# Sums of x stored halfway between steps, four first products of expert 0 made ahead of the groups, weight sums placed behind a group's first product

## The chip, the core and the metric

The kernel runs on one core of a Trainium2 chip. The metric is the device time of one execution in microseconds (us). The kernel before the change took 2215.28 us (median of 3 runs, 2215.21 to 2216.24).

## The reference, cut to what matters

Three stages follow each other. All numbers are float32.

```python
# 1. delta-rule attention, 32 heads, 768 steps, head size 48 -> x [3072, 384]
# 2. mixture of 8 experts, dense, weighted by a balanced table P
logits = x @ w_gate;  P = exp(logits - logits.max())
for _ in range(8):
    P /= P.sum(1, keepdims=True) + 1e-09      # rows
    P /= P.sum(0, keepdims=True) + 1e-09      # columns
    P *= N / E
for e in range(E):
    h = np.maximum(x @ w1[e], 0.0)            # 384 -> 1024
    out += P[:, e:e+1] * (h @ w2[e])          # 1024 -> 384
# 3. h = x @ w_in;  out = (h * cos(h)) @ w_out   (384 -> 2048 -> 384)
```

## The kernel before, in words

**Precision.** Each float32 factor is split into two rounded parts (hi, lo), and a product is three or four matmuls of 128x128 weights by 512 tokens. So TensorE has most of the work.

**Attention and expert 0.** The function `tick` walks through strings of letters (`SEQ`), one letter per piece of work, in the order in which the engines get them. A letter `m` is a half step of expert 0: `moe0_h(s)` (nine matmuls into one bank, then `relu_split`: ScalarE rounds, VectorE subtracts) or `moe0_y(s)` (nine matmuls into the three banks `yb`). These halves stand in the list `mq`. When attention ends, 14 are left: a loop issues nine of them with the first steps of the balancing of P (`sk_some`), and five go into the groups.

**Groups.** Experts 1 to 7 run over pairs of token blocks: three pairs (p), 28 groups each, 84 groups (n) in all. Instead of x the groups use seven tiles T0 to T6 of sums and differences of x's blocks. `group(n)` makes seven products (`mm`, four matmuls each: T0 and T5 first, into banks A_ and G_, then T4, T1, T3, T2, T6) and four small ones (`zz`, with the third part of T1 or T6), copies banks on ScalarE, and makes four relus. Between them, at four places `F()`, it issues one piece of nine matmuls into `yb` from the groups before. After the first of these, `gates` reads the three banks `yb` on VectorE, multiplies by the expert's row of P, and GpSimd adds the result to the accumulator.

**Weights of the next group.** `s_prep(n + 1)` gives six steps q0 to q5: q0 is four sums on GpSimd (lines 1042 to 1045), q1 to q3 and q5 round on ScalarE and subtract on VectorE, q4 is four sums on GpSimd.

**Hand-over.** In the last group of a pair (n = 27 and 55) each T tile is loaded anew behind its last product (`tl`, `t_load`). All these loads go through SyncE's queue, in the order in which the code issues them, with the raw weights of the group after the next (`g_load`, lines 1007 and 1008).

**Sums of x.** `t_prep(p)` makes the T tiles of a pair and stores them to `tsc`. Its steps k0 to k7 load parts of x, add, subtract, and `emit` (ScalarE rounds into slot 4, line 897; VectorE puts the rest into slot 5, line 898). What a step makes is stored only when the next step begins (line 956), right ahead of that step's own work; a last empty step stores what is left. For p = 0 the steps are in `tq`, popped by `tick` at every fourth letter; for p = 1 and 2 they are in `bgq`, which a group pops at three places (`bg`): after the second `zz`, ahead of q5, and at its end. Each step is followed by an empty place. Behind them `bgq` holds 32 conversions of the last stage's weights (`cv`): p0 loads (lines 1160, 1163), two empty places, then p1, p2, p3 on VectorE (lines 1167 to 1179), and p3 stores to `wsn` (lines 1184 to 1191).

Of the kernel before, what the change touches and what calls it, by code (L numbers as in the profile page):

```python
# [9 lines left out]
F32R = mybir.dt.float32r  # L10
# [25 lines left out]
def kernel(  # L36
# [13 lines left out]
    nc = tc.nc  # L50
# [575 lines left out]
    def moe0_h(s):  # L626
        m, f = divmod(s, FT)

        bank = pa[0] if scr and s % 2 and not grp else hb
        h_mms(bank, f // 2, f, xb[m], 0, 512)  # L630
        h = hp.tile([128, 2, 512], F32R, tag="h", name="h")
        relu_split(h, bank, 512)
        h0_t[s] = h

# [10 lines left out]
    NS0 = NB * FT  # L645
# [6 lines left out]
    with tc.manual_schedule():  # L652
# [108 lines left out]
        n = [gk_n(2, pcd)]  # L761
# [17 lines left out]
        nc.scalar.activation(out=wg[:, :, 0, :], in_=wg_sb, func=ACTF.Copy)  # L779


        scr, grp = [], []

        mq = [(2, lambda: moe0_h(0))]
        for s in range(NS0):
# [6 lines left out]
        def half():  # L792
            if mq and mq[0][0] <= done[0]:
                mq.pop(0)[1]()
# [9 lines left out]
        def tick(u, seq):  # L804
            early = u < 2
            for x, c in enumerate(seq.split()):
                inv_some(3)
                if x % 4 == 3 and tq:
                    tq.pop(0)()
                if len(c) == 2:  # L810
                    u, c = int(c[1]), c[0]
                if c == "m":
                    half()
                elif c == "K":
                    pe_KS(u)
                elif c == "k":
                    pe_QS(u)
                elif c in "ZY":
                    pe_Z1(u, *([p01[:, 0]] if early else []))
                elif c in "zy":  # L820
                    pe_Z2(u, *([p01[:, 1]] if early else []))
                elif c == "U":
                    pe_U(u)
                    load_v(u + 2)
                elif c == "S":
                    pe_S(u)
                    load_k(u + 5)
                elif c == "P":
                    pe_PU(u)
                elif c == "T":  # L830
                    n = take(c)
                    if n is not None:
                        pe_TK(n)
                elif c == "B":
                    n = take(c)
                    if n is not None:
                        pe_GK(n)
                elif c == "N":
                    n = take(c)
                    if n is not None:  # L840
                        pe_N(n)
                elif c == "Q":
                    n = u if early else u + 1
                    if n < NU:
                        pe_TQ(n, p23 if early else pcd)
                        load_q(n + 1)
                elif c == "q":
                    n = u if early else u + 1
                    if n < NU:
                        pe_GQ(n, p01 if early else pab)  # L850
                elif c == "E":
                    pe_TQ(u)
                    load_q(u + 1)
                elif c == "e":
                    pe_GQ(u)
                elif c == "X":
                    pe_XT(u, p23 if early else pcd)
                    done[0] = u + 1
                elif c == "r" and u + 1 < NU:
                    inv_some(99)  # L860
                    inv_dm(Xsys)
                elif c == "R" and u + 1 < NU:
                    inv_tx(Xsys)
                elif c == "i" and u + 2 < NU:
                    inv_q.extend(inv_ops(Nst, Nsys, Xsys, tmp, nc.gpsimd))
                elif c in "Gg":
                    (pe_gate if c == "G" else pe_gate2)((u - 1) // 2)
                elif c in "ab":
                    w_half(0, "ab".index(c))
                    if c == "b":  # L870
                        w_load(1)
                elif c == "W":
                    n = take(c)
                    w_split(n)
                    if n + 1 < NG:
                        w_load(n + 1)
# [9 lines left out]
        def t_prep(p, sl, add):  # L886

            b0, b1 = 2 * p, 2 * p + 1
            s = [sl(i) for i in range(6)]
            g, v, later = add, nc.vector.tensor_tensor, []  # L890

            def ld(i, b, a, k):
                nc.sync.dma_start(out=s[i], in_=xs(b, a, k))

            def emit(i, src):
                hi, lo = s[4].bitcast(F32R), s[5].bitcast(F32R)
                nc.scalar.activation(out=hi, in_=src, func=ACTF.Copy)
                v(out=lo, in0=src, in1=hi.bitcast(F32), op=ALU.subtract)
                later.append((tsc[p][i, :, 0, :], s[4]))
                later.append((tsc[p][i, :, 1, :], s[5]))  # L900

            def corr(i, a, b, op, slot):
                o = s[slot].bitcast(F32R)
                v(out=o, in0=a, in1=b, op=op)
                later.append((tsc[p][i, :, 2, :], s[slot]))
                return o.bitcast(F32)

            def k0():
                ld(0, b1, 0, 0), ld(1, b1, 1, 0), ld(2, b0, 0, 0), ld(3, b0, 1, 0)

            def k1():
                g(out=s[0], in0=s[0], in1=s[1], op=ALU.add)
                g(out=s[2], in0=s[2], in1=s[3], op=ALU.add)
                ld(1, b1, 0, 1), ld(3, b1, 1, 1)

            def k2():
                v(out=s[2], in0=s[0], in1=s[2], op=ALU.subtract)
                emit(3, s[2])
                g(out=s[1], in0=s[1], in1=s[3], op=ALU.add)
                ld(3, b0, 1, 1)  # L920

            def k3():
                v(out=s[0], in0=s[1], in1=s[0], op=ALU.subtract)
                emit(5, s[0])
                ld(0, b0, 0, 1)

            def k4():
                v(out=s[1], in0=s[1], in1=s[2], op=ALU.subtract)
                emit(4, s[1])
                g(out=s[0], in0=s[0], in1=s[3], op=ALU.add)  # L930
                ld(2, b0, 1, 2), ld(3, b1, 1, 2)

            def k5():
                v(out=s[0], in0=s[0], in1=s[1], op=ALU.subtract)
                emit(2, s[0])
                ld(0, b0, 0, 2), ld(1, b1, 0, 2)

            c = {}

            def k6():  # L940
                for i, j in ((1, 0), (6, 1)):
                    o = s[j].bitcast(F32R)
                    nc.scalar.activation(out=o, in_=s[j], func=ACTF.Copy, scale=1.0 / 4096)
                    later.append((tsc[p][i, :, 2, :], s[j]))
                    c[i] = o.bitcast(F32)
                c[3] = corr(3, s[3], s[2], ALU.subtract, 4)

            def k7():
                corr(5, c[6], s[3], ALU.subtract, 5)
                c[4] = corr(4, c[6], c[3], ALU.subtract, 3)  # L950
                corr(2, c[1], c[4], ALU.subtract, 2)

            def step(f):
                def run():
                    for o, i in later:
                        nc.sync.dma_start(out=o, in_=i)
                    later.clear()
                    f()
                return run

            return [step(f) for f in (k0, k1, k2, k3, k4, k5, k6, k7, lambda: None)]

        tick(0, SEQ[0])
        tick(2, SEQ[1])
# [163 lines left out]
        sq = s_prep(0)  # L1128
        lead = [[], [], [], [sq[0]], [sq[1]], [sq[2]], [sq[3]], [sq[4]], [sq[5]]]
        nb = 0  # L1130
        while len(mq) > 5:
            for x in lead.pop(0) if lead else []:
                x()
            half()
            nb += 1
            if nb in (1, 2, 4, 6, 8):
                sk_some()
# [145 lines left out]
        def group(n):  # L1283
# [10 lines left out]
            def tl(i):  # L1294
                if swap:
                    t_load(p + 1, i)
# [8 lines left out]
            tl(0)  # L1305
            if n and n + 2 < NGR:
                g_load(n + 2)
            mm(G_, n, 5, True)
            tl(5)
            copy(B_, A_)  # L1310
            while late and late[0][0] <= n:
# [2 lines left out]
            skp(n)  # L1314
            gates()
            copy(s7, G_)
            nx[0]()
            mm(A_, n, 4)
            tl(4)
            if last:  # L1320
# [193 lines left out]
                net_b3(j - 1)  # L1514


        grp.append(1)
        skb[0] = hb
        for bank in (B_, D_):
            nc.tensor.matmul(  # L1520
                out=bank, lhsT=s_hi(0, 0), rhs=Tt[0][:, 0, :], start=True, stop=True, skip_group_check=True
            )
        fill.extend(lambda: half() for _ in range(len(mq)))
        group(0)
        tpv = tpt.rearrange("p a (s c) -> p (a s) c", c=512)
        for p in range(1, NP):
            for x in t_prep(p, lambda i: tpv[:, i, :], nc.gpsimd.tensor_tensor):
                bgq.extend([x, lambda: None])
        bgq.extend(cv)
        for n in range(1, NGR):  # L1530
            group(n)
# [69 lines left out]
```

## Time and profile before

| | value |
|---|---|
| median of 3 runs | 2215.28 us |
| the profiled execution's own time | 2210.57 us |
| its span, first to last instruction | 2208.9 us |
| TensorE busy | 2129.0 us, 96% of the span |
| VectorE, ScalarE, GpSimd busy | 1432.6, 997.5, 1087.2 us |
| TensorE busy in 400 to 600 us (end of attention, first groups) | 187.4 of 200 us |
| TensorE busy in 800 to 1600 us (groups, two hand-overs) | 793.5 of 800 us |

The page gives busy times over the whole span. Since TensorE is busy 96% of it, what matters is where it is not: the waits of TensorE by the line that waits and what released it, and in the timeline what stood in the way there. A matmul's record overlaps the next one's, so a row of eight matmuls that takes 1.98 us gives them 0.23 us each. The same row with a longer time shows matmuls at the lower granted clock: in 480 to 490 us the mean granted clock is 0.83 of full speed, in 490 to 500 us it is 1.00.

### The profile page before, as it was taken

The numbers are of one execution on the slowest core, as the hardware profiler recorded it, in microseconds if no ns is written. First come the engines' busy times: TensorE is split into PE (matmuls) and PEld (weight loads), VectorE is DVE, ScalarE is ACT, GpSimd is POOL, SyncE is SP. The second block draws the span as 40 slices with busy tenths as digits, with TensorE's granted clock in tenths as the row PEclk, the third lists the DMA queues.
The fourth block names the chain that finished last, engine by engine and source line by source line (L and its number), as shares of the span: only waits on it lengthen the run. The fifth ranks groups of instructions, "written<-read, shape, count | busy, mean of one in ns | idle before, by whom it ended". The sixth has DMA issues, their size and how long they took to land.

```text
span 2208.9 us, 40836 instructions
## 1 busy us (share of the span) xinstructions
PE 2129.0 (96%) x16359; PEld 1778.2 (81%) x16359; DVE 1432.6 (65%) x2289; ACT 997.5 (45%) x1819; POOL 1087.2 (49%) x1507
## 2 busy tenths in 40 slices
PE   6889999889999999999999999999999999999998
PEld 5677777677878888788888887888888888888888
DVE  6555544376566777677777776777776546666665
ACT  2333332244444444444444444444444446666665
POOL 4656544426655556565555565655555532222221
PEclk8889999999999999999999999999999999999999
DMA  4432323544442224522222236222222260000000
GB/s 85 103 81 67 81 57 91 189 173 128 138 137 95 71 92 119 199 91 92 92 87 89 71 116 217 90 79 92 91 82 74 67 271 17 13 29 29 15 15 15
DMA packets 217374, 206.66 MB, mean 94 GB/s; under 512 B 83952, under 2 KB 193040, under 8 KB 217184
## 3 DMA queue, kind: packets, MB, share of 16 engines
q1 hardware_dynamic: 213840, 197.16, 28.8%
q0 software_dynamic: 2176, 6.60, 0.9%
q8 instruction: 128, 2.10, 0.4%
q14 instruction: 62, 0.51, 0.1%
q10 hardware_dynamic: 1168, 0.30, 0.1%
HBM read 156.71 MB, written 47.28 MB: 92 GB/s over the span
## 4 chain that ended last, share of the span: by engine, by line
PE 84%; DVE 7%; DMA 4%; ACT 2%; issue 2%; POOL 1%; SPq 1%; DVEq 0%; POOLq 0%; ACTq 0%
PE ps L145 31%; PE ps L1212 22%; PE ps L1459 9%; PE ps L1418 8%; PE ps L133 4%; PE ps L1217 3%; DMA T<-tsc 2%; PE ps L459 1%; PE ps L273 1%; PE ps L247 1%; DVE mh L152 1%; PE ps L441 1%; PE ps L429 1%; PE ps L487 1%; DMA tsc<-tp 0%
## 5 line engine op out<-in xcount | busy, mean ns | idle before, releaser
L145 PE MATMUL ps<-mh,w2t 128*128 128x512 f32 x3024 | 742.5, 390 | 0.6 <-DVE ct L1248 0.5
L145 PEld LDWEIGHTS ps<-mh,w2t 128*128 128x128 f32 x3024 | 568.6, 188 | 120.8 <-DVE ct L1248 2.9
L1212 PE MATMUL ps<-T,w1t 128*128 128x512 f32 x2352 | 594.3, 392 | 10.7 <-DMA T<-xsc 4.8
L1212 PEld LDWEIGHTS ps<-T,w1t 128*128 128x128 f32 x2352 | 443.0, 189 | 106.1 <-ACT ps L1222 5.9
L1249 POOL TENSOR_TENSOR accp<-accp,ct 128x512 f32<-128x512 f32 x252 | 327.3, 1328 | 329.8 <-DVE ct L1248 329.7
L152 DVE SCALAR_TENSOR_TENSOR mh<-ps,mh 128x512 fp32r<-128x512 f32 x168 | 115.2, 686 | 264.4 <-ACT mh L151 264.4
L1222 ACT ACTIVATE ps<-ps 128x512 f32<-128x512 f32 x168 | 97.8, 582 | 309.5 <-PE ps L1212 238.2
L1248 DVE TENSOR_TENSOR ct<-ps,scr 128x512 f32<-128x512 f32 x252 | 158.2, 683 | 81.6 <-PE ps L145 78.3
L1222 ACT ACTIVATE ct<-ps 128x512 f32<-128x512 f32 x168 | 100.5, 598 | 244.0 <-PE ps L1212 243.9
L1427 POOL TENSOR_SCALAR tp<-tp 128x512 f32<-128x512 f32 x96 | 60.1, 626 | 247.2 <-ACT tp L1426 247.0
L1079 POOL TENSOR_TENSOR w1t<-w1t 128x128 fp32r<-128x128 f32 x84 | 62.9, 749 | 222.8 <-DVE w1t L1065 204.4
L1441 DVE TENSOR_TENSOR tp<-tp,ps 128x512 f32<-128x512 f32 x96 | 66.1, 688 | 144.8 <-ACT tp L1440 144.8
L151 ACT ACTIVATE mh<-ct 128x512 fp32r<-128x512 f32 x168 | 106.1, 632 | 101.9 <-DVE ct L1347 56.7
L152 DVE SCALAR_TENSOR_TENSOR mh<-ct,mh 128x512 fp32r<-128x512 f32 x168 | 144.6, 861 | 0.4 <-ACT mh L151 0.3
L1459 PE MATMUL ps<-w1t,h 128*128 128x384 f32 x600 | 136.8, 341 | 4.3 <-DVE h L1451 2.8
L133 PE MATMUL ps<-xb,w1t 128*128 128x512 f32 x432 | 116.4, 413 | 6.1 <-ACT xb L539 2.7
L1217 PE MATMUL ps<-T,w1t 128*128 128x512 f32 x336 | 118.8, 393 | 1.7 <-DMA T<-tsc 1.7
L1459 PEld LDWEIGHTS ps<-w1t,h 128*128 128x128 f32 x600 | 107.2, 189 | 12.5 <-DVE h L1451 5.4
L145 PE MATMUL ps<-h,w2t 128*128 128x512 f32 x432 | 113.2, 407 | 0.0
L352 POOL TENSOR_TENSOR w1t<-w1t 128x30 f32<-128x30 f32 (+9 forms) x180 | 99.1, 551 | 14.1
L133 PEld LDWEIGHTS ps<-xb,w1t 128*128 128x128 f32 x432 | 80.9, 194 | 26.8 <-DVE xb L540 3.5
L151 ACT ACTIVATE mh<-ps 128x512 fp32r<-128x512 f32 x168 | 98.5, 587 | 0.6 <-PE ps L1217 0.6
(272 smaller groups left out, 3445.8 us busy)
## 6 DMA issues: line engine op xcount, KB each, us to landing
scr<-in_moe_w_dram SPq DMA_DIRECT2D x84, 384.0 KB
raw<-in_moe_w_dram SPq DMA_DIRECT2D x84, 384.0 KB
wsn<-tp SPq DMA_DIRECT2D x64, 192.0 KB
scr<-pts SPq DMA_DIRECT2D x45, 256.0 KB
xsc<-xb SPq DMA_DIRECT2D x24, 384.0 KB
T<-tsc SPq DMA_DIRECT2D x12, 768.0 KB
tsc<-tp SPq DMA_DIRECT2D x28, 256.0 KB
tp<-xsc SPq DMA_DIRECT2D x24, 256.0 KB
```

What stands on the lines that cost most here:

```text
L133: nc.tensor.matmul(out=ps[:, :nn], lhsT=w[:, a, kk, fs], rhs=x[:, b, kk, c0:c0 + nn], start=(i == 0), stop=(i == 3 * KD - 1),)
L145: nc.tensor.matmul(out=banks[kd], lhsT=w[:, a, f % 2, kd * 128:(kd + 1) * 128], rhs=h[:, b, :], start=(first and b == 0 and a == 0), stop= ...
L151: nc.scalar.activation(out=h[:, 0, :nn], in_=ps[:, :nn], func=ACTF.Relu)
L152: nc.vector.scalar_tensor_tensor(out=h[:, 1, :nn], in0=ps[:, :nn], scalar=0.0, in1=h[:, 0, :nn].bitcast(F32), op0=ALU.max, op1=ALU.subtract,)
L352: eng.tensor_tensor(out=xsys[:, j + 1:, 0:j], in0=xsys[:, j + 1:, 0:j], in1=a, op=ALU.add)
L1212: nc.tensor.matmul(out=bank, lhsT=a, rhs=b, start=start and q == 0, stop=stop and q == 3, skip_group_check=True)
L1217: nc.tensor.matmul(out=bank, lhsT=s_z(n, f), rhs=Tt[(1, 6)[t]][:, 2, :], start=False, stop=True, skip_group_check=True)
L1222: nc.scalar.activation(out=out, in_=in_, func=ACTF.Copy)
L1248: nc.vector.tensor_tensor(out=c, in0=yb[kd], in1=pslot[t], op=ALU.mult)
L1249: nc.gpsimd.tensor_tensor(out=a[:, kd, :], in0=a[:, kd, :], in1=c, op=ALU.add)
L1418: nc.tensor.matmul(out=hb2(i), lhsT=net_w1(f, a, kk), rhs=x2[b](c, kk), start=(j == 0), stop=(j == 3 * KD - 1))
L1459: nc.tensor.matmul(out=ybk[t][:, :DM], lhsT=h[:, a, ts], rhs=net_w2(f, c), start=(f == 0 and j == 0), stop=(f == FT2 - 1 and j == 2),)
```

## The change

- `t_prep` no longer stores at the start of the next step: every step is followed by a `flush` of its own that issues the stores. `tick` pops at every second letter in place of every fourth; in `bgq` the flush takes the empty place.
- The 14 halves left of expert 0 are put in another order: the last four first products (s = 44 to 47) come ahead of the groups, each into a bank of its own, with their h in the groups' tiles `mh`; what is left for the groups is five second halves.
- In `group`, q0 (`nx[0]`) moves from behind `gates` to the place between the group's first and second product. The first product into bank D_ that only opens the bank (`seed`) moves from ahead of group 0 into it.

```diff
-        bank = pa[0] if scr and s % 2 and not grp else hb
+        if s >= NS0 - 4:
+            bank, h = (pa[2], pa[1], pa[0], hb)[s % 4], htile()
+        else:
+            bank = pa[0] if scr and s % 2 else hb
+            h = hp.tile([128, 2, 512], F32R, tag="h", name="h")
         h_mms(bank, f // 2, f, xb[m], 0, 512)
-        h = hp.tile([128, 2, 512], F32R, tag="h", name="h")
...
-                if x % 4 == 3 and tq:
+                if x % 2 == 1 and tq:
                     tq.pop(0)()
...
-            def step(f):
-                def run():
-                    for o, i in later:
-                        nc.sync.dma_start(out=o, in_=i)
-                    later.clear()
-                    f()
-                return run
-
-            return [step(f) for f in (k0, k1, k2, k3, k4, k5, k6, k7, lambda: None)]
+            def flush():
+                for o, i in later:
+                    nc.sync.dma_start(out=o, in_=i)
+                later.clear()
+
+            return [x for f in (k0, k1, k2, k3, k4, k5, k6, k7) for x in (f, flush)]
...
+        z = NS0 - 8
+        order = [("y", z), ("h", z + 2), ("y", z + 1), ("h", z + 3), ("y", z + 2)]
+        order += [("h", s) for s in range(NS0 - 4, NS0)] + [("y", s) for s in range(z + 3, NS0)]
+        mq[:] = [(0, lambda c=c, s=s: (moe0_h if c == "h" else moe0_y)(s)) for c, s in order]
         while len(mq) > 5:
...
+            nx[0]()
             mm(G_, n, 5, True)
+            if n == 0:
+                seed(D_)
             tl(5)
...
             copy(s7, G_)
-            nx[0]()
             mm(A_, n, 4)
...
             for x in t_prep(p, lambda i: tpv[:, i, :], nc.gpsimd.tensor_tensor):
-                bgq.extend([x, lambda: None])
+                bgq.append(x)
         bgq.extend(cv)
```

**Place one: SyncE's queue at the first hand-over (group 27).** `T_6388` is T0, `T_6389` T5, `T_6390` T4, `T_6391` T3, `T_6392` T2, `T_6393` T1, `T_6394` T6; `wsn` are the stores of a conversion's p3, `tp<-in_moe_w` the load of a p0, `scr` and `raw` a group's raw weights. Before:

```order
L1189 DMA wsn_76<-tp 128x384 x2
L1094 DMA T_6388<-xsc_71 128x2x512
L1099 DMA T_6388<-xsc_71 128x512
L1007 DMA raw_6400<-in_moe_w_dram 128x3x256
L1008 DMA raw_6400<-in_moe_w_dram 128x2x384
L1101 DMA T_6389<-tsc_96 128x1536
L1101 DMA T_6390<-tsc_96 128x1536
L1163 DMA tp<-in_moe_w_out_dram 128x768
L1101 DMA T_6391<-tsc_96 128x1536
```

And of the change, at the same place:

```order
L1008 DMA scr<-in_moe_w_dram 128x2x384
L1094 DMA T_6388<-xsc_71 128x2x512
L1099 DMA T_6388<-xsc_71 128x512
L1007 DMA raw_6400<-in_moe_w_dram 128x3x256
L1008 DMA raw_6400<-in_moe_w_dram 128x2x384
L1101 DMA T_6389<-tsc_96 128x1536
L1101 DMA T_6390<-tsc_96 128x1536
L1101 DMA T_6391<-tsc_96 128x1536
```

The conversions stand four places earlier in `bgq` (32 places for `t_prep` in place of 36), so that other parts of them fall into group 27: the stores are no longer ahead of T0, and the load of the next conversion no longer between T4 and T3. It is the same at group 55.

**Place two: TensorE from the last halves ahead of the groups into group 0.** L133 is a first product of expert 0, L145 a second, L597 the product of a step of the balancing. Before:

```order
L597 MATMUL ps_99<-small,ones 128x8
L145 MATMUL ps_99<-h,w2t 128x512 x9
L1520 MATMUL ps_99<-T_6388,w1t 128x512 x2
L1212 MATMUL ps_99<-T_6388,w1t 128x512 x4
L1212 MATMUL ps_99<-T_6389,w1t 128x512 x4
L133 MATMUL ps_99<-xb,w1t 128x512 x9
L597 MATMUL ps_99<-small,ones 128x8
L1212 MATMUL ps_99<-T_6390,w1t 128x512 x4
```

And of the change:

```order
L597 MATMUL ps_99<-small,ones 128x8
L133 MATMUL ps_99<-xb,w1t 128x512 x9
L1526 MATMUL ps_99<-T_6388,w1t 128x512
L1217 MATMUL ps_99<-T_6388,w1t 128x512 x4
L1217 MATMUL ps_99<-T_6389,w1t 128x512 x4
L1526 MATMUL ps_99<-T_6388,w1t 128x512
L145 MATMUL ps_99<-h,w2t 128x512 x9
L597 MATMUL ps_99<-small,ones 128x8
L1217 MATMUL ps_99<-T_6390,w1t 128x512 x4
```

In group 0 a second half now stands where a first one stood, so nothing but the balancing writes bank hb there.

**Place three: GpSimd in group 2.** L1119 is the accumulator by P, L1249 the adds of `gates`, L1042 to L1045 the sums q0. Before:

```order
L1119 TENSOR_TENSOR accp_6396<-accp_6396,scr 128x1536
L1249 TENSOR_TENSOR accp_6396<-accp_6396,ct 128x512 x3
L1042 TENSOR_TENSOR ct<-raw_6400 128x128
L1043 TENSOR_TENSOR ct<-ct,raw_6400 128x128
L1044 TENSOR_TENSOR ct<-raw_6400 128x128
L1045 TENSOR_TENSOR ct<-raw_6400,ct 128x128
```

And of the change:

```order
L1042 TENSOR_TENSOR ct<-raw_6400 128x128
L1043 TENSOR_TENSOR ct<-ct,raw_6400 128x128
L1044 TENSOR_TENSOR ct<-raw_6400 128x128
L1045 TENSOR_TENSOR ct<-raw_6400,ct 128x128
L1119 TENSOR_TENSOR accp_6396<-accp_6396,scr 128x1536
L1254 TENSOR_TENSOR accp_6396<-accp_6396,ct 128x512 x3
```

The four sums have moved from behind six blocks of 128x512 to ahead of them.

## Rows read from the trace of the kernel before

**Rows 1.** Waits of TensorE, whole span: waiting line, releaser, us in total, times, longest

```profile
PE ps L1212 <- DMA T<-xsc: 4.8, 2, 2.7
PE ps L273 <- ACT QT L260: 4.9, 2, 3.8
PE ps L1212 <- ACT ps L1222: 4.7, 3, 2.0
PE ps L597 <- DVE h L152: 3.5, 2, 2.1
```

**Rows 2.** Timeline, first hand-over: start, us, engine, line, operation, tiles, count, [idle before]

```profile
891.73 1.98 PE L1212 MATMUL ps<-T,w1t 128*128 128x512 f32 x8
892.17 4.26 SPq L1189 DMA_DIRECT2D wsn<-tp  x2
896.52 0.53 SPq L1094 DMA_DIRECT2D T<-xsc  x1
897.85 2.20 PE L145 MATMUL ps<-mh,w2t 128*128 128x512 f32 x9
900.07 0.65 SPq L1163 DMA_DIRECT2D tp<-in_moe_w_out_dram  x1
...
910.99 1.07 PE L1212 MATMUL ps<-T,w1t 128*128 128x512 f32 x4
914.78 1.91 PE L1212 MATMUL ps<-T,w1t 128*128 128x512 f32 x4 [2.72 <-DMA T<-xsc]
...
917.62 0.77 PE L1217 MATMUL ps<-T,w1t 128*128 128x512 f32 x1 [0.51 <-DMA T<-tsc]
918.18 2.35 PE L145 MATMUL ps<-mh,w2t 128*128 128x512 f32 x9
```

**Rows 3.** Timeline, second hand-over, TensorE

```profile
1347.64 1.07 PE L1212 MATMUL ps<-T,w1t 128*128 128x512 f32 x4
...
1354.15 4.04 PE L145 MATMUL ps<-mh,w2t 128*128 128x512 f32 x9
1357.99 2.35 PE L1212 MATMUL ps<-T,w1t 128*128 128x512 f32 x8
```

**Rows 4.** Busy times by stretch: ..., granted clock, DMA share, GB/s

```profile
900.00:916.00 16.00, 13.28 (x57) 10.64 (x56) 11.86 (x17) 7.21 (x14) 9.67 (x13) 0.97 1.02 393
```

**Rows 5.** Timeline, groups 0 and 1, TensorE and VectorE

```profile
460.31 0.39 PE L597 MATMUL ps<-small,ones 128*128 128x8 f32 x2 [1.41 <-DVE h L152]
463.11 0.52 DVE L594 TENSOR_REDUCE small<-P 128x8 f32<-128x192 f32 x1
481.07 0.39 PE L597 MATMUL ps<-small,ones 128*128 128x8 f32 x2 [1.77 <-DVE small L594]
481.31 3.60 PE L1212 MATMUL ps<-T,w1t 128*128 128x512 f32 x8
```

**Rows 6.** Timeline, groups 2 and 3, ScalarE and TensorE

```profile
511.44 0.63 ACT L1072 ACTIVATE w1t<-ct 128x512 fp32r<-128x512 f32 x1 [4.90 <-POOL ct L1045]
513.66 1.16 PE L1212 MATMUL ps<-T,w1t 128*128 128x512 f32 x4 [0.99 <-DVE ct L1347]
518.83 3.62 PE L1212 MATMUL ps<-T,w1t 128*128 128x512 f32 x8 [1.95 <-ACT ps L1222]
```

**Rows 7.** Timeline, end of attention, SyncE's queue and ScalarE

```profile
390.00 1.24 SPq L956 DMA_DIRECT2D tsc<-kr  x2
394.43 0.63 ACT L897 ACTIVATE kr<-kr 128x512 fp32r<-128x512 f32 x1 [5.87 <-DMA tsc<-kr]
```

**Rows 8.** Timeline, VectorE from the end of a group to the next

```profile
908.21 0.68 DVE L152 SCALAR_TENSOR_TENSOR mh<-ps,mh 128x512 fp32r<-128x512 f32 x1
910.74 1.89 DVE L1248 TENSOR_TENSOR ct<-ps,scr 128x512 f32<-128x512 f32 x3 [1.85 <-PE ps L145]
...
914.38 1.51 DVE L1169 SCALAR_TENSOR_TENSOR tp<-tp 128x384 f32<-128x384 f32 x1
```

**Rows 9.** Groups by line, whole span: count, busy us, mean ns, idle before

```profile
L1042 POOL TENSOR_TENSOR ct<-raw 128x128 f32<-128x128 f32 x42 | 29.0, 691 | 7.1 <-DMA raw<-in_moe_w_dram 7.1
```

More of the change, by code (lines that the diff above doesn't have):

```diff
@@ L779 @@
         nc.scalar.activation(out=wg[:, :, 0, :], in_=wg_sb, func=ACTF.Copy)
-        scr, grp = [], []
+        scr = []
         mq = [(2, lambda: moe0_h(0))]
@@ L1130 @@
         nb = 0
+        assert len(mq) == 14
+        z = NS0 - 8
+        order = [("y", z), ("h", z + 2), ("y", z + 1), ("h", z + 3), ("y", z + 2)]
+        order += [("h", s) for s in range(NS0 - 4, NS0)] + [("y", s) for s in range(z + 3, NS0)]
+        mq[:] = [(0, lambda c=c, s=s: (moe0_h if c == "h" else moe0_y)(s)) for c, s in order]
         while len(mq) > 5:
@@ L1514, in net_step, with seed @@
                 net_b3(j - 1)
-        grp.append(1)
         skb[0] = hb
-        for bank in (B_, D_):
+        def seed(bank):
             nc.tensor.matmul(
@@ L1522 @@
             )
+        seed(B_)
         fill.extend(lambda: half() for _ in range(len(mq)))
```

## The prediction

> **What bounds the kernel now.** I read the page's shares first: TensorE is busy nearly all the time, and the change adds and removes no matmul. So only three things can move the end: TensorE's waits, matmuls at the lower clock, and new waits. The list of TensorE's waits comes next [rows 1]. The largest that bear on this change are: 4.8 us on loads of T tiles, in two places; 4.9 us on ScalarE's copy of QT, of which one wait has 3.8; 4.7 us on ScalarE's copy of a bank; and 3.5 us on the VectorE part of an h. Last the timeline of each of these places, to see what stands behind the releaser that is named.
>
> **Part by part.**
>
> *Hand-overs (groups 27 and 55).* T0 is free when the first four matmuls of 891.73 are done, at about 892.7. Its load leaves SyncE at 896.52, because the queue stands at the two `wsn` stores (892.17, 4.26 us long), whose second waits for VectorE's end of a conversion [rows 2]. So all seven loads start 3.8 us late. Then the load of the next conversion's 384 KB (900.07) goes between T4 and T3. The DMA engines are full there, at 393 GB/s [rows 4], so these bytes cost 1.0 us. The product with T1 waits 2.72 us, and the one with the third part of T6 another 0.51 [rows 2]. From 910.99 to 918.18 TensorE issues ten matmuls. Eight take 1.98 us (891.73), ten thus at most 2.5, so 4.7 us are lost. In the second hand-over the same ten take 1347.64 to 1354.15, 4.0 lost, and then nine matmuls take 4.04 in place of 2.20 and eight 2.35 in place of 1.98: another 2.2 [rows 2, 3]. Together 10.9.
> The order of SyncE's queue in the change has neither the stores ahead of T0 nor the load between T4 and T3. The loads then land up to 3.8 + 1.0 = 4.8 us earlier. The last that is needed, the third part of T6, came at 917.62. Without a stall it is due nine matmuls after 910.99, at 913.2, so it is 4.4 us late: the 4.8 just cover it. What could spoil this is that the DMA engines run dry before T3 may be loaded. Four loads of 768 KB (786,432 bytes) take 8.0 us at 393 GB/s, from 892.7 to 900.7; T3's load leaves after 900.07, so they hardly do. I take 10.5 of the 10.9. The lower bound is 2 (the 1.0 us of the conversion's load, twice), the upper 10.9.
>
> *Groups 0 and 1.* The two waits of 3.5 us in all are for the h that two first products leave in bank hb, which the balancing also uses [rows 1]. The change makes these two products ahead of the groups, in other banks, and their nine matmuls each are replaced by nine of a second half, so the work stays. Next in line is the balancing itself. From a product at 460.31 its chain on VectorE ends at 463.11 + 0.52, so 3.3 us later [rows 5]. Three of its products have more than that between them, filled by other matmuls. But two have VectorE's relus and splits ahead of their chain, and 481.07 waits 1.77 us for that today. That order is not changed. I leave 1.4 us of this wait and add 0.8 for the product before, which now comes sooner: 2.2 left of 5.2, a gain of 3.0. The eight matmuls behind the wait take 3.60 us in place of 1.98, at the lower of the two clock levels (1.2 for 2.4 GHz); with shorter waits ahead I take it that the clock stays: 1.6. Together 4.6; bounds 0 (the waits only move) and 6.8 (all go).
>
> *Groups 2 and 3.* ScalarE stood 4.90 us for q0's sums on GpSimd, which came behind the accumulator's multiply and three adds [rows 6]. From there everything on ScalarE and VectorE was late: 0.99 us before T5's product, 1.95 before T4's, and eight matmuls of 3.62. With q0 first on GpSimd this wait of ScalarE is gone. What is late next is step k2, whose rounding stands in ScalarE's queue ahead of the copy that T4's product needs; from durations I get 1.2 us of wait left. Gain 1.7 of the waits and 1.6 of the clock, 3.3. Bounds 0 and 4.5.
>
> *Later steps of the sums.* The bank-copy wait has two more places, 4.7 - 1.95 = 2.75 us [rows 1]. Both have a step with an `emit` in the last of a group's three places, close ahead of that copy. The earlier stores don't help there: the copy waits for VectorE's subtraction ahead of the rounding, not for a store. Of p = 1 one such step stays. Those of p = 2 move by two places, so two fall there in place of one. At 0.7 us each, three make 2.1: gain 0.6. Bounds -3.3 (three at the longest of rows 1, 2.0 us, against 2.75) and 2.7.
>
> *End of attention.* The 3.8 us wait comes from ScalarE: it stands 5.87 us at line 897 for two stores that left SyncE at 390.00, right behind the stores of x itself [rows 7]. In the change the steps come two letters earlier and their stores between steps. But the flush behind k3 is popped behind letter X, and its stores are again behind x's own in SyncE's queue; k4's rounding waits for them, and the copy of QT now stands right behind that rounding. So the stall has a new owner and the same end: 0. Bounds -1.0 (x's rounding now waits for the stores of k2, too) and +3.8.
>
> *All 84 groups, 32 conversions.* With q0 early GpSimd works beside VectorE's end of the group, and p1 falls to that end in place of the middle. VectorE ends its group at 908.89 and then waits 1.85 us for the piece whose banks `gates` reads. The next piece writes these banks ten matmuls later (2.3 us), and the first of the three operations of `gates` takes 0.6, so `gates` may begin some 1.7 us after 910.74, at 912.4. A p1 of 3.3 us (912.63 to 915.89 beside the adds of `gates`) fits from 908.89 to 912.2 [rows 8]. Cost 0; bounds 0 and what the fourth rival says.
> One of the three operations of p1, line 1169, takes 1.51 us on 384 columns while GpSimd adds; line 152 takes 0.68 on 512 [rows 8]. The Trainium skill (SBUF — State Buffer, Who interferes with whom) says that a VectorE instruction with two inputs in SBUF and a GpSimd instruction that reads SBUF shut each other out, the later one fully. The trace agrees in the 1.51. By that rule q0 beside a group's end delays what VectorE has left there, which is the fourth rival's mechanism.
>
> **Sum.** 10.5 + 4.6 + 3.3 + 0.6 = 19.0 us. From the profiled execution's own 2210.57 (span 2208.9 and 1.7 around it) that gives 2191.6. The median is 4.7 above that execution, so the forecast is 2215.28 - 19.0, rounded, 2196.5 us. A change counts as one from 0.2%, 4.4 us: about what a measurement of this kernel can tell.
>
> **Rivals.**
> 1. *The hand-overs stay bound by their bytes.* Then only the 1.0 us of the conversion goes, twice: 19.0 - 8.5 = 10.5, 2205. For it: the DMA engines are full for 16 us at a stretch [rows 4]. Against: they are idle while SyncE stands at the stores.
> 2. *Groups 0 to 3 only move their waits.* VectorE's chain of the balancing sets these groups whatever TensorE issues, and the low clock stays: only 10.5 + 0.6 is left, 2204. For it: 481.07 waits for that chain already. Against: the two other waits name an h, not the chain.
> 3. *The stall at the end of attention goes as well,* since the stores of k2 and k3 leave earlier than I have them: 19.0 + 3.8 and some 2 us of slow matmuls behind it, 2190.5.
> 4. *Slower: the end of the group on VectorE.* Four sums of q0 at 0.69 us [rows 9] shut VectorE out for up to 2.8 us there. With p1 `gates` would then start up to 2.6 us past 912.4, and TensorE waits at bank `yb` 32 times: up to 83 us, 2280. It takes 0.6 us past the limit (19 over 32) to eat the gain up; from 0.8 on it is slower. For it: the page's rule. Against: p1's 3.3 us were measured beside GpSimd's adds already, and q0 is over before the most of p1.
> 5. *Nothing moves,* the gains being slack elsewhere: 2215.
>
> **How the numbers follow.** Forecast 0.48, rival 1 0.17, rival 2 0.13, rival 3 0.08, rival 4 0.07, rival 5 0.07. The range 2190 to 2211 holds the forecast (2191 to 2202 by its bounds), rivals 1 to 3, and leaves out 4 and 5. Faster: 0.48 + 0.17 + 0.13 + 0.08 = 0.86; within 0.2%: 0.07; slower: 0.07.
>
> **What would show it.** At both hand-overs T0's load leaves within 1 us of the end of its product, and TensorE's wait for T is under 0.5 us; if the wait stays at 2 us or more, rival 1 has it. In group 0 no wait names an h; in group 1 one wait of 1 to 2 us for the balancing stays, with 1.98 us for the eight matmuls behind it. In group 2 ScalarE's line 1072 has no wait for GpSimd. At the end of attention a wait of 3 to 4 us for QT stays. In the groups with a p1, TensorE's wait for `gates` is zero; waits of tenths there, many times over, would be rival 4. The prediction is wrong if TensorE's busy time in 800 to 1600 us doesn't rise, or if the time is above 2211 us.

## The result: 2194.03 us, 1% faster, and the profile after

| | before | after |
|---|---|---|
| median (runs) | 2215.36 us (4, 2215.21 to 2216.24) | 2194.03 us (4, 2191.07 to 2196.56) |
| ratio | | 0.9905, 95% interval 0.9891 to 0.9919 |
| profiled execution, its span | 2210.57, 2208.9 us | 2193.01, 2191.3 us |
| VectorE, GpSimd busy | 1432.6, 1087.2 us | 1472.8, 1168.6 us |
| TensorE busy in 800 to 1600 us | 793.5 of 800 us | 799.3 of 800 us |

The gain is 21.3 us by the medians and 17.6 us between the two profiled executions. The forecast was 19.0 us, 2196.5 us.

First TensorE's waits of after over the whole span, as in [rows 1] (`mm` is now line 1217, `zz` 1222, the bank copy 1227, `gates` 1253):

```profile
PE ps L273 <- ACT QT L260: 5.6, 2, 4.5
...
PE ps L597 <- DVE small L594: 2.7, 3, 1.1
...
PE ps L1217 <- ACT ps L1227: 1.8, 2, 1.7
```

No wait is put down to a T tile any more, and none to an h in the balancing. The wait for QT has grown. The timeline of the first hand-over (SyncE's queue, then TensorE), which answers to [rows 2]:

```profile
883.91 0.53 SPq L1094 DMA_DIRECT2D T<-xsc  x1
884.54 0.55 SPq L1099 DMA_DIRECT2D T<-xsc  x1
...
883.04 1.98 PE L1217 MATMUL ps<-T,w1t 128*128 128x512 f32 x8
...
904.83 0.47 PE L1222 MATMUL ps<-T,w1t 128*128 128x512 f32 x1 [0.32 <-ACT w1t L1052]
```

T0's product is the first half of the eight matmuls of 883.04, over at about 883.9, and its load leaves right there. In before 3.8 us lay between. The only wait is 0.32 us. The profile names line 1052, but what that line makes there is a weight of the next group, which this product doesn't read; it reads the third part of T6. In a second profile of the change ("again" in the table below) the same product at the second hand-over names the load:

```profile
1337.99 0.47 PE L1222 MATMUL ps<-T,w1t 128*128 128x512 f32 x1 [0.57 <-DMA T<-tsc]
```

So T6's last part is still late by a few tenths of a us.

Groups 1 to 3 of after, TensorE and ScalarE, against [rows 5, 6]:

```profile
475.05 0.39 PE L597 MATMUL ps<-small,ones 128*128 128x8 f32 x2 [1.14 <-DVE small L594]
480.49 0.39 PE L597 MATMUL ps<-small,ones 128*128 128x8 f32 x2 [1.07 <-DVE small L594]
480.73 2.10 PE L1217 MATMUL ps<-T,w1t 128*128 128x512 f32 x8
500.11 2.62 PE L145 MATMUL ps<-mh,w2t 128*128 128x512 f32 x9 [0.89 <-DVE ct L1253]
504.65 0.63 ACT L1072 ACTIVATE w1t<-ct 128x512 fp32r<-128x512 f32 x1
513.99 2.11 PE L1217 MATMUL ps<-T,w1t 128*128 128x512 f32 x8 [0.15 <-ACT ps L1227]
```

The balancing's own chain is what is late now, 1.1 us twice. Line 1072 has no wait (4.90 before), and the eight matmuls that took 3.60 and 3.62 us take 2.1.

The end of attention in after (TensorE, ScalarE, SyncE's queue), against [rows 7]:

```profile
400.82 1.98 PE L273 MATMUL ps<-QT,KT 48*64 48x64 f32 x64 [4.47 <-ACT QT L260]
402.73 4.21 PE L133 MATMUL ps<-xb,w1t 128*128 128x512 f32 x9
...
399.23 0.63 ACT L900 ACTIVATE kr<-kr 128x512 fp32r<-128x512 f32 x1 [5.62 <-DMA tsc<-kr]
...
392.63 0.92 SPq L542 DMA_DIRECT2D xsc<-xb  x2
393.59 1.89 SPq L958 DMA_DIRECT2D tsc<-kr  x2
```

The stores of k3 stand behind those of x, k4's rounding waits 5.62 us for them, and QT's copy stands behind that: the new owner of the stall that the prediction named.

**Where the time went, group by group.** Each group rounds the next weights once on ScalarE (line 1049), so these rows are a clock. First and last of one stretch, from the weights of group 26 to those of group 30, before and then after:

```profile
866.36 0.30 ACT L1049 ACTIVATE w1t<-scr 128x128 fp32r<-128x128 f32 x1
...
933.08 0.30 ACT L1049 ACTIVATE w1t<-scr 128x128 fp32r<-128x128 f32 x1
```

```profile
857.67 0.30 ACT L1049 ACTIVATE w1t<-scr 128x128 fp32r<-128x128 f32 x1
...
919.89 0.30 ACT L1049 ACTIVATE w1t<-scr 128x128 fp32r<-128x128 f32 x1
```

That is 66.72 and 62.22 us for four groups. From group 30 to 54 both kernels take 369.92 us, 15.413 a group. What a stretch takes above 15.413 a group is its loss. The table has it in us, from one profile of each kernel; by how much a hand-over can scatter is seen below, under prep_early (the runs are described below; "again" is the change a second time):

| weights of group | before | after | again | phase_only | phase_back | q0_back | order_back | flush_back | stores_later |
|---|---|---|---|---|---|---|---|---|---|
| 0 to 2 | 7.4 | 3.4 | 3.4 | 6.7 | 3.4 | 4.1 | 6.6 | 3.4 | 3.4 |
| 2 to 4 | 7.9 | 3.1 | 3.0 | 6.7 | 3.1 | 7.4 | 2.9 | 2.5 | 2.8 |
| 4 to 26 | 4.9 | 2.2 | 2.3 | 6.5 | 2.4 | 2.1 | 2.3 | 6.6 | 2.4 |
| 26 to 30 | 5.1 | 0.6 | 0.7 | 5.0 | 7.4 | 2.6 | 0.9 | 1.5 | 1.9 |
| 30 to 54 | 0.0 | 0.0 | 0.0 | 1.2 | 0.3 | 1.2 | 0.0 | 0.0 | 0.4 |
| 54 to 58 | 6.4 | 0.6 | 0.9 | 2.4 | 8.0 | 1.2 | 0.7 | 1.4 | 2.4 |
| 58 to 83 | 0.0 | 0.0 | 0.0 | 1.2 | 0.4 | 1.2 | 0.0 | 0.0 | 0.4 |
| sum | 31.6 | 9.9 | 10.2 | 29.7 | 24.9 | 19.8 | 13.4 | 15.4 | 13.7 |

The groups give 31.6 - 9.9 = 21.7 us, as much as the medians. The 17.6 us of the profiles is smaller because after's execution was 2.7 us later when the groups began (448.2 for 445.5 us at the first of these rows) and took 1.4 us longer behind the last. The first 390 us scatter from execution to execution: the last transposition of x in attention that comes before 400 us (line 534) starts at 390.10 us in one profile of the change and at 391.67 in another, and their groups agree to 0.3 us in each stretch.

### The profile page after: what moved, and what is told of

Read it like the earlier page. It is cut to its first block, busy times and chain, and to the rows that moved or that the text cites. A ratio compares the mean times of both kernels' runs of the same rounds, so it can differ in the third digit from the quotient of the medians.

```text
span 2191.3 us, 40894 instructions
## 1 busy us (share of the span) xinstructions
PE 2123.1 (97%) x16359; PEld 1777.6 (81%) x16359; DVE 1472.8 (67%) x2289; ACT 990.0 (45%) x1819; POOL 1168.6 (53%) x1507
## 3 DMA queue, kind: packets, MB, share of 16 engines
q1 hardware_dynamic: 213840, 197.16, 29.7%
## 4 chain that ended last, share of the span: by engine, by line
PE 87%; DVE 6%; POOL 2%; ACT 2%; issue 2%; DMA 1%; DVEq 0%; POOLq 0%; SPq 0%; ACTq 0%
PE ps L145 33%; PE ps L1217 23%; PE ps L1466 9%; PE ps L1425 8%; PE ps L133 4%; PE ps L1222 3%; PE ps L459 1%; PE ps L273 1%; PE ps L247 1%; PE ps L441 1%; PE ps L429 1%; PE ps L487 1%; DVE mh L152 1%; POOL bw L677 0%; DMA tsc<-kr 0%
## 5 line engine op out<-in xcount | busy, mean ns | idle before, releaser
L145 PE MATMUL ps<-mh,w2t 128*128 128x512 f32 x3060 | 749.4, 390 | 0.9 <-DVE ct L1253 0.9
L145 PEld LDWEIGHTS ps<-mh,w2t 128*128 128x128 f32 x3060 | 574.2, 188 | 121.3 <-DVE ct L1253 2.8
L1254 POOL TENSOR_TENSOR accp<-accp,ct 128x512 f32<-128x512 f32 x252 | 335.4, 1359 | 97.5 <-DVE ct L1253 97.4
L152 DVE SCALAR_TENSOR_TENSOR mh<-ct,mh 128x512 fp32r<-128x512 f32 x168 | 154.0, 917 | 0.4 <-ACT mh L151 0.3
L133 PE MATMUL ps<-xb,w1t 128*128 128x512 f32 x432 | 118.9, 420 | 6.0 <-ACT xb L539 2.7
L133 PEld LDWEIGHTS ps<-xb,w1t 128*128 128x128 f32 x432 | 82.6, 199 | 27.2 <-DVE xb L540 3.5
L145 PE MATMUL ps<-h,w2t 128*128 128x512 f32 x396 | 103.8, 408 | 0.0
```

Of the source, the lines that this page charges most:

```text
L133: nc.tensor.matmul(out=ps[:, :nn], lhsT=w[:, a, kk, fs], rhs=x[:, b, kk, c0:c0 + nn], start=(i == 0), stop=(i == 3 * KD - 1),)
L145: nc.tensor.matmul(out=banks[kd], lhsT=w[:, a, f % 2, kd * 128:(kd + 1) * 128], rhs=h[:, b, :], start=(first and b == 0 and a == 0), stop= ...
L152: nc.vector.scalar_tensor_tensor(out=h[:, 1, :nn], in0=ps[:, :nn], scalar=0.0, in1=h[:, 0, :nn].bitcast(F32), op0=ALU.max, op1=ALU.subtract,)
L1254: nc.gpsimd.tensor_tensor(out=a[:, kd, :], in0=a[:, kd, :], in1=c, op=ALU.add)
```

## The experiments

Ratios are to the kernel before, run on the same chip.

**phase_only.** Only the conversions' places are those of the change:

```
-            cv.extend([p0, lambda: None, lambda: None, p1, p2, p3])
+            cv.extend([p0] + [lambda: None] * (1 if len(cv) < 20 else 2) + [p1, p2, p3])
```

> The kernel before, with four empty places fewer among its first four conversions, so that from the fifth conversion on all stand where they stand in the change; nothing else of the change is in it. Theory A (SyncE's queue stood at the stores ahead of T0's load): the whole hand-over term comes, 10.5 us, about 2205, T0's load leaves within 1 us of its product and TensorE's wait for T is under 0.5 us at both hand-overs. Rival B (the loads are bound by their bytes): 2 us, 2213, and waits of 2 us stay. Rival C (what went is due to the earlier q0 or the new order of halves as well): under 8 us.

Measured 2209.13 us, ratio 0.9972 (0.9961 to 0.9984). Of the waits for T those for T6's third part are left, 1.9 and 1.0 us. But 1.39 us more are lost in each of four groups (26, 30, 54, 58) where nothing was lost before. VectorE, GpSimd and TensorE there, in this run:

```profile
879.28 3.74 DVE L1179 SCALAR_TENSOR_TENSOR tp<-tp 128x384 fp32r<-128x384 int32 x1
...
878.79 3.81 POOL L1119 TENSOR_TENSOR accp<-accp,scr 128x1536 f32<-128x1536 f32 x1
...
885.74 2.62 PE L145 MATMUL ps<-mh,w2t 128*128 128x512 f32 x9 [0.62 <-DVE ct L1248]
```

A step of the conversion's p3 has two inputs in SBUF. It begins 0.5 us into GpSimd's 3.81 us multiply of the accumulator and ends only 0.4 us behind it; `gates` is then late. In the change (VectorE, GpSimd) the early q0 keeps the multiply back until p3 is over:

```profile
868.07 0.70 DVE L1184 SCALAR_TENSOR_TENSOR tp<-tp 128x384 fp32r<-128x384 int32 x1
...
871.06 3.51 POOL L1119 TENSOR_TENSOR accp<-accp,scr 128x1536 f32<-128x1536 f32 x1
```

The Trainium skill (SBUF — State Buffer, Who interferes with whom) has such a pair shut each other out, the later one fully; the 3.74 us here against 0.70 in the change agrees.

So the new places alone bring less than theory A has, as rival C says (6.1 us by the medians, though the interval, 3.5 to 8.6, reaches past its 8). Of the 8.6 us by which this run loses more than the change from group 26 on, 4.9 are this multiply beside p3, and there the early q0 is what makes the places free. The rest stands at T6's third part: its waits, and at the first hand-over nine matmuls at the lower clock behind one (3.73 us in place of 2.20). Why that part lands later here, with the same order in the queue, no run shows. The table's sums differ by only 1.9 us between this run and before; where the other 4 us of the medians come from is open.

**phase_back.** The reverse:

```
+        bgq.extend([lambda: None] * 4)
         bgq.extend(cv)
```

> The change with four empty places put ahead of the conversions, so that these stand where they stood before. Theory A: 10.5 us slower than the change, about 2205, with waits of 2 to 3 us for T at both hand-overs again. Rival B: at most 2 us slower, 2196. If p1 at a group's end cost anything in the change, it comes back here and the loss is smaller than 10.

Measured 2205.58 us, ratio 0.9962 (0.9950 to 0.9975): 11.6 us slower than the change. SyncE's queue and TensorE's waits at the first hand-over:

```profile
880.37 4.93 SPq L1194 DMA_DIRECT2D wsn<-tp  x2
885.39 0.54 SPq L1094 DMA_DIRECT2D T<-xsc  x1
...
903.23 1.19 PE L1217 MATMUL ps<-T,w1t 128*128 128x512 f32 x4 [2.96 <-DMA T<-xsc]
906.09 0.77 PE L1222 MATMUL ps<-T,w1t 128*128 128x512 f32 x1 [1.33 <-DMA T<-tsc]
```

Theory A holds. The hand-overs lose 7.4 and 8.0 us, more than in before (5.1, 6.4): here q0 runs beside the VectorE work in front of p3's end, line 1088 takes 1.21 us in place of 0.95, and the stores wait longer.

**stores_later.** As phase_back, but p3's stores go into a list that the next p0 issues:

```
             def p0():
+                while stq:
+                    o, i = stq.pop(0)
+                    nc.sync.dma_start(out=o, in_=i)
...
-                        nc.sync.dma_start(out=wsn[g][:, 1, r * DM:r * DM + DM], in_=t)
+                        stq.append((wsn[g][:, 1, r * DM:r * DM + DM], t))
```

> The change with four empty places ahead of the conversions, as in the run that put them back, and with the stores of a conversion issued only with the next conversion's load, when their data are long there. The bytes at the hand-overs are the same or more; only SyncE's queue does not stand still ahead of T0's load. Theory A (the queue's wait is what costs): T0's load leaves within 1 us of its product, the four groups from 26 on take 62.5 to 65 us in place of 69.1, the same at the second hand-over, about 2196. Rival B (the loads are bound by their bytes): 68 us or more, 2205.

Measured 2193.97 us, ratio 0.9902 (0.9886 to 0.9917), as fast as the change. SyncE's queue:

```profile
885.97 0.54 SPq L1094 DMA_DIRECT2D T<-xsc  x1
...
888.31 2.08 SPq L1101 DMA_DIRECT2D T<-tsc  x2
890.44 1.28 SPq L1167 DMA_DIRECT2D wsn<-tp  x2
891.78 0.58 SPq L1173 DMA_DIRECT2D tp<-in_moe_w_out_dram  x1
894.41 1.23 SPq L1101 DMA_DIRECT2D T<-tsc  x2
```

T0's load leaves as its product ends (885.10 and four matmuls of 0.23 us). More bytes than before stand between T4 and T3, and still the hand-overs lose only 1.9 and 2.4 us, 5.5 and 5.6 less than in phase_back. So most of it was the standing queue and not the bytes. The 1.3 and 1.8 us above the change are somewhat less than stores and load would cost there by their bytes (an estimate: 768 KB take 2.0 us at the 393 GB/s of [rows 4]).

**q0_back.** q0 again behind `gates`:

```
-            nx[0]()
             mm(G_, n, 5, True)
...
             copy(s7, G_)
+            nx[0]()
             mm(A_, n, 4)
```

> The change with the four sums of q0 behind gates again. Theory: ScalarE's wait of about 5 us in group 2 comes back, with 2 to 3 us of waits and 1.6 us of slow matmuls on TensorE: 3.3 us slower than the change, about 2197.5. Rival (the early stores of the steps alone had taken that wait): no difference, 2194. Rival (q0 beside VectorE's end of the group costs in each group): faster than the change, and GpSimd's busy time falls by 80 us, VectorE's by 40.

Measured 2202.50 us, ratio 0.9945 (0.9930 to 0.9960): 8.5 us slower than the change, where the theory had 3.3. GpSimd's busy time does fall, to 1087.1 us, but nothing is won by it. ScalarE's wait of group 2 is back:

```profile
510.38 0.63 ACT L1072 ACTIVATE w1t<-ct 128x512 fp32r<-128x512 f32 x1 [4.91 <-POOL ct L1045]
```

By the table 4.3 us return in groups 2 to 4, and in groups 26, 30, 54 and 58 the same 1.39 us as in phase_only, less 0.17 made up in each group behind: 4.9 in all. The theory didn't have these.

**mul_split.** q0_back, with the accumulator's multiply in three pieces:

```
-            nc.gpsimd.tensor_tensor(
-                out=acc(p, t), in0=acc(p, t), in1=pzero[t][:, None, :].to_broadcast([128, KD, 512]), op=ALU.mult
-            )
+            for kd in range(KD):
+                nc.gpsimd.tensor_tensor(
+                    out=acc(p, t)[:, kd, :], in0=acc(p, t)[:, kd, :], in1=pzero[t], op=ALU.mult
+                )
```

> The change with q0 behind gates, as in the run that put it back, and with GpSimd's multiply of the accumulator by P made in three instructions of 128x512 in place of one of 128x1536. In that run one VectorE operation of a conversion took 3.74 us beside this multiply and TensorE then waited 0.63 us for gates, in group 26 and 54. Theory (the long GpSimd instruction shuts VectorE out until it ends): the VectorE operation takes at most 1.9 us, both waits of 0.63 us are gone, and 1 to 2 of the 8 us come back, about 2201. Rival (VectorE is slow there for another reason, or the three shut it out as one): 3 us or more, and the waits stay.

One run, 2201.45 us. VectorE, GpSimd and TensorE of group 26:

```profile
872.23 1.53 DVE L1185 SCALAR_TENSOR_TENSOR tp<-tp 128x384 fp32r<-128x384 int32 x1
873.68 2.04 DVE L1088 TENSOR_TENSOR w2t<-scr,w2t 128x768 fp32r<-128x768 f32 x1
875.64 1.77 DVE L152 SCALAR_TENSOR_TENSOR mh<-ct,mh 128x512 fp32r<-128x512 f32 x1
...
871.74 5.13 POOL L1120 TENSOR_TENSOR accp<-accp,scr 128x512 f32<-128x512 f32 x3
...
878.67 2.62 PE L145 MATMUL ps<-mh,w2t 128*128 128x512 f32 x9 [0.61 <-DVE ct L1254]
```

The theory's first part held, the operation is shorter. Its second part fell: now three operations stand (5.3 us together, where q0_back has 5.4), GpSimd takes longer, and TensorE's wait stays. The rows read as the two engines taking turns, instruction by instruction, so cutting the multiply smaller gave nothing back here (20.4 us lost in the groups, 19.8 in q0_back); moving it away, as in the change, did.

**order_back.** The 14 halves, their banks and the seeds as before, the rest of the change kept:

```
...
-        mq[:] = [(0, lambda c=c, s=s: (moe0_h if c == "h" else moe0_y)(s)) for c, s in order]
...
-            if n == 0:
-                seed(D_)
...
         seed(B_)
+        seed(D_)
```

> The change with the 14 halves in the order of before and both seeds ahead of group 0. Theory: waits of 1.4 us for an h in group 0 and of 1.8 us in group 1 and slow matmuls behind them come back: 4.6 us slower than the change, about 2198.5. Rival (only the balancing's own chain counts): 0 to 1 us.

Measured 2195.54 us, ratio 0.9912 (0.9899 to 0.9925): 1.5 us slower than the change by the medians, which the intervals don't tell apart, and 3.2 us in groups 0 to 2 by the table, where the theory had 4.6. The waits for an h are back, and of the balancing's own one of 0.5 us is left:

```profile
466.48 0.39 PE L597 MATMUL ps<-small,ones 128*128 128x8 f32 x2 [1.41 <-DVE h L152]
477.70 0.56 PE L597 MATMUL ps<-small,ones 128*128 128x8 f32 x2 [2.04 <-DVE h L152]
```

**flush_back.** Stores at the start of the next step (`step` flushes, then works), with the groups' places unchanged and attention popping at every fourth letter as before:

```
-                if x % 2 == 1 and tq:
+                if x % 4 == 3 and tq:
...
-            return [x for f in (k0, k1, k2, k3, k4, k5, k6, k7) for x in (f, flush)]
...
+            if p == 0:
+                return [step(f) for f in (k0, k1, k2, k3, k4, k5, k6, k7, lambda: None)]
+            fl = [lambda: None] * 7 + [flush]
+            return [x for f, y in zip((k0, k1, k2, k3, k4, k5, k6, k7), fl) for x in (step(f), y)]
```

> The change with the stores of a step issued at the start of the next step again; attention pops at every fourth letter as before; in the groups the places of all steps and conversions stay as in the change. Theory of the prediction: the flush itself brings nothing, the end of attention takes the same within 1 us and TensorE's wait for QT there is 3.8 us; the groups 8 to 26 stay at 277.9 us, since it was the two places by which the second pair's steps moved that took a wait of 2.0 us there: 2194. Rival (the earlier stores took that wait): 280 us in groups 8 to 26, and 2196 to 2197.

Measured 2197.17 us, ratio 0.9920 (0.9907 to 0.9934). The total alone wouldn't settle it, but the stretch does, and the rival was right: groups 8 to 26 take 280.74 us (before 280.68, after 277.86), and with groups 4 to 8 it is 4.3 us. ScalarE and TensorE of this run, then ScalarE of the change at the same step:

```profile
618.01 0.63 ACT L900 ACTIVATE tp<-tp 128x512 fp32r<-128x512 f32 x1 [4.81 <-DMA tsc<-tp]
...
628.49 2.12 PE L1226 MATMUL ps<-T,w1t 128*128 128x512 f32 x8 [1.74 <-ACT ps L1236]
```

```profile
612.24 0.61 ACT L900 ACTIVATE tp<-tp 128x512 fp32r<-128x512 f32 x1
```

A late store holds this rounding back, the next step's rounding comes later (627.32 in place of 623.57 us, 2.9 us of it against the groups' clock), and at 628.49 us TensorE waits 1.74 us for the bank copy. It is the same in before, at ScalarE and then TensorE:

```profile
622.62 0.63 ACT L897 ACTIVATE tp<-tp 128x512 fp32r<-128x512 f32 x1 [4.74 <-DMA tsc<-tp]
...
633.38 2.14 PE L1212 MATMUL ps<-T,w1t 128*128 128x512 f32 x8 [2.02 <-ACT ps L1222]
```

The wait for QT is 3.8 us in flush_back, as expected.

**prep_early, raw_early, best, best2: attempts at more, and the change again.** prep_early begins the first pair's sums three pops sooner (ten empty pops of the 13 in the tick before):

```
-            if u == NU - 2:
...
+            if u == NU - 3:
...
+                tq.extend([lambda: None] * 10)
```

> The change with the steps of the first pair's sums begun three pops earlier in attention, so that k4 and its flush come before letter X and ahead of the letter that copies QT there stands only a flush. Theory (TensorE's wait of 4.5 us for QT comes from k4's rounding, which waits on ScalarE for stores queued behind those of x): the wait falls under 1 us and the nine matmuls behind it take 2.3 in place of 4.2 us, 5 to 6.5 us faster than the change, about 2188. Rival (the stall only moves to another step, or ScalarE is late there anyway): within 1.5 us of the change, 2194.

Measured 2192.09 us, ratio 0.9898 (0.9881 to 0.9916): not to be told from the change. The long wait for QT is gone (one of 1.1 us, which the change has too, stays), two others have come, at TensorE:

```profile
394.07 2.35 PE L133 MATMUL ps<-xb,w1t 128*128 128x512 f32 x9 [1.78 <-DVE h L152]
...
404.98 1.96 PE L459 MATMUL ps<-S,KT 48*64 48x48 f32 x64 [2.24 <-DVE Pp L328]
...
907.03 0.47 PE L1223 MATMUL ps<-T,w1t 128*128 128x512 f32 x1 [1.33 <-DMA T<-tsc]
```

The last row is the first hand-over: the groups have the same code as in the change, and yet T6's third part is 1.33 us late and the four groups lose 2.0 us, where the change's two profiles lose 0.6 and 0.7.

raw_early issues `g_load` of a pair's last group at the end of the group before it:

```
-            if n and n + 2 < NGR:
+            if n and n + 2 < NGR and not swap:
                 g_load(n + 2)
...
+            if (n + 2) % GP == 0 and n + 3 < NGR:
+                g_load(n + 3)
             relu(n, 1, 1, s4)
```

> The change, with the two loads of raw weights (384 KB) that stand in SyncE's queue between T0 and T5 at the hand-overs issued at the end of the group before, when the DMA engines are idle. Theory (in the change the loads of T are bound by their bytes, and T6's last part lands at the very time it is needed): the 1.0 us of these bytes goes out of the way, no wait for T is left, and the four groups from 26 and from 54 on take 61.7 to 62.3 us: 0.5 to 1 us a hand-over less than the change where that has a wait, 2193. Rival (the lateness of T6 is set by when T6 comes free and by the loads behind it): 62.2 to 63.6 us as before, waits of 0.5 to 1.4 us for T's third part.

Measured 2191.02 us, ratio 0.9902 (0.9883 to 0.9921). Its hand-overs lose 0.0 and 0.4 us, in sum the least of all runs, and the wait at T6's third part is gone at both (best and best2, with the same early loads, keep one of 0.3 to 0.4 us each). So in the change that part lands at about the moment it is needed; the 0.2 to 0.6 us a hand-over that the early loads bring here are too small for the total to show.

best is both of these together:

> The raw weights early as in the run beside it, and the sums of the first pair three pops earlier in attention. If both terms stand by themselves: 2 to 3 us faster than the change, about 2191. Rival: nothing, 2194, if what the earlier sums give is lost again in the wait for VectorE's part of an h and for Pp.

Measured 2192.11 us, ratio 0.9902 (0.9885 to 0.9918). The two do not add up to anything that the total shows.

best2 adds to best an empty place ahead of the second pair's steps (its last flush shares the place of the third pair's k0, so that all behind stays):

```
...
+            if p == 1:
+                bgq.append(lambda: None)
...
```

> As the run beside it, and the steps of the second pair's sums one place later, so that k2 and k5 stand at a group's end in place of k4 and k1, as they do for the third pair, where no wait was seen. Theory: the wait of 1.7 us for ScalarE's copy of a bank in groups 4 to 8 goes: 63.4 to 61.9 us, 2189.5. Rival: k2 at the end of group 2 costs as much there: 2 us more in groups 2 to 4, 2191.

Measured 2192.04 us, ratio 0.9898 (0.9881 to 0.9914). Both theory and rival hold: groups 4 to 26 lose 1.3 in place of 2.2, but groups 2 to 4 lose 5.8 in place of 3.1.

The change itself:

> The change itself, for its time on the same chip as the three others and for what differs between two executions of it: 2194 by the runs so far. If the first 390 us differ by some us from the profiled execution shown while the groups take the same to 0.1 us, the scatter between runs comes from there. If T6's last part is late by about 1 us in one hand-over, its landing is at the edge.

Measured 2190.75 us, ratio 0.9896 (0.9881 to 0.9911); line 534 and the stretches as said above. On the same chip raw_early, best and best2 took 2191.0 to 2192.1 us, so no version tried is shown to beat the change.

## Why the prediction was right, point by point

- *Hand-overs, 10.5 us.* Measured 5.1 + 6.4 - 0.6 - 0.6 = 10.3. T0's load left at the end of its product, the wait at T6's third part is 0.3 to 0.6 us in the change's two profiles (the prediction had its 4.8 us just cover the 4.4), and stores_later shows that the queue's stand was most of the cause; rival 1 is out. That the term agrees to 0.2 us is in part luck: in prep_early, with the same groups, the hand-overs lose 2.0 + 0.7 us, which would make it 8.8. And the prediction missed that the term doesn't stand alone. Without the early q0 the new places lose 4.9 us again (phase_only, q0_back); q0 had been moved for groups 2 and 3, so that it pays for this was luck, too.
- *Groups 0 and 1, 4.6.* Measured 7.4 - 3.4 = 4.0; the new order by itself 3.2. The waits that stay are 1.1 and 1.1 us at two products of the balancing, where 0.8 and 1.4 were expected, and one of 0.5 us.
- *Groups 2 and 3, 3.3.* Measured 7.9 - 3.1 = 4.8, above the prediction's own bound of 4.5: it had counted two waits and one slow row, 4.5 us, where the stretch lost 7.9. The early q0 by itself is 4.3. ScalarE's wait went; of the 1.2 us that were to be left at T4's product 0.15 was. The new 0.89 us are for `gates`.
- *Later steps of the sums, 0.6.* Measured 4.9 - 2.2 = 2.7. This step of the prediction was wrong in its reason, not only its size. It said that earlier stores don't help there, because the copy waits for VectorE's subtraction, not for a store. That holds for the rounding right in front of the copy; but one step earlier a rounding waits for late stores (4.74 us in before), and with these stores put back (flush_back, 4.81 us) groups 8 to 26 lose what they lost in before. Nor are three waits of 0.7 us left: the second pair's steps keep one, of 1.67 us, the third pair's none.
- *End of attention, 0.* The wait for QT went from 3.8 to 4.47 us, with the owner that was named, so rival 3 is out. From the last row of line 534 to the first row of the groups' clock it is 58.6 us in before, 58.1 in phase_only, which has none of the change's edits there, and 58.1 and 57.2 in the change: no loss, and a gain of about a us can't be told from the scatter.
- *84 groups, 0.* Groups 30 to 54 take the same 369.92 us. The fourth rival's mechanism is real, but what costs time is GpSimd's long multiply and not q0, and there the early q0 helps. Beside q0 VectorE is longer as well (some 20 us of busy time in all, see the end), without a loss at TensorE. VectorE is still in time for `gates` behind a p1, by waiting for TensorE itself (VectorE, first hand-over):

```profile
917.23 0.70 DVE L1174 SCALAR_TENSOR_TENSOR tp<-tp 128x384 f32<-128x384 f32 x1
918.11 1.89 DVE L1253 TENSOR_TENSOR ct<-ps,scr 128x512 f32<-128x512 f32 x3 [0.18 <-PE ps L145]
```

- *The sum.* 4.0 + 4.8 + 2.7 + 10.3 = 21.8 of the groups against 19.0: the mis-sized terms are the later steps (2.1 too small), groups 2 and 3 (1.5 too small) and groups 0 and 1 (0.6 too large). Together they leave the forecast gain 2.8 us below the groups' and 2.3 below the medians'.

## What to carry to other kernels

Look at what stands ahead of a load in the queue that issues it: a store whose data come late delays every load behind it, and issuing the stores later gave the hand-overs 11.1 us of the 14.2 that the new places give against phase_back. Terms of a sum that are worked out one by one need a second look together: here one edit paid for what another would have cost. And where a loop repeats, take the start of one instruction a round as a clock; the distance between such rows showed a tenth of a us where the total scatters by several.

## What the runs showed of the hardware that was not expected

- One VectorE instruction of 128x384 took 3.74 us beside a 3.81 us GpSimd multiply, and 0.56 to 0.70 us elsewhere. In three pieces the multiply took 5.13 us, and VectorE's loss stayed the same (one run).
- The change made GpSimd busy for 81 us more and VectorE for 40 us more (table at the top); with q0 back it is 1087.1 and 1452.1 us, so q0 has all of the one and half of the other. It cost TensorE nothing: 24 groups take 369.92 us in before and after.
- The first 390 us, with few edited instructions in them, differ by several us between executions: line 534 starts at 386.89 us in before, and in other profiles of this study from 388.04 to 396.90. The mean granted clock of the first 200 us is 0.86 in before, the earliest, and 0.81 in raw_early, the latest; that this is the cause wasn't tested.
